# Two sums of a Strassen step in PSUM, split inputs of the second run by transfer, and a new placing of weight blocks and restores

## The chip, the cores and the metric

The kernel runs on one core of a Trainium2 chip. The metric is the device time of one execution in microseconds (us), taken as the median of several runs.

## The reference, cut to what matters

Three steps follow each other. The first is a retention (attention without softmax, with a decay by head) over q, k, v of 4 x 8 x 576 x 64, which gives x with 2304 rows of 512. The other two are:

```
h = x @ w_in                        # 512 -> 2048
g = where(h > 0, h, exp(min(h, 0)) - 1)
x = g @ w_out                       # 2048 -> 512
gate = 1 / (1 + exp(-(x @ w_gate))) # 512 -> 1536
val = x @ w_val
out = gate * val @ w_o2             # 1536 -> 512
```

The weights come in double precision, and the kernel works in single precision throughout.

## The kernel before, in words

**Numbers.** Every operand of a matmul is a pair of a high and a low part: ScalarE (ACT) copies the number to the high part, and VectorE (DVE) or GpSimd (POOL) subtracts it for the low part. A product takes three matmuls: high by high, high by low, low by high. A weight block comes from DRAM as words of doubles and is turned into such a pair on the chip by a chain of steps (`Weight.chain`): ACT, L149 and L150; DVE, L152, L153, L156 and L158; then the split, ACT L104 and POOL L105.

**Rows of x.** They lie in five groups: 0 to 3 with 512 columns each, group 4 with 256. Groups 0 and 1 form a pair, and so do 2 and 3.

**The unit.** For a pair and two column blocks of weights, `unit` does a 2 by 2 Strassen-Winograd step: seven products P1, P7, P6, P2, P5, P3, P4, in this order, of six 128x512 matmuls each, in three PSUM banks A, D, B, and eight sums. Its sums need three weight combinations in an `s` tile (`Sums.chain`, L188 to L192) and, for the pair, the split x pieces "11", "21", "22", "t1" to "t4" (`Pair`: `sum` at L436, `high` at L440, `low` at L444). The sums spoken of below are c22 (L493, from s4 and bank D), c21 (L505, from s2 and bank D), and the copy of A to B at L474. After a unit of the first feed-forward layer, `elu` finishes each of four results: two ACT steps (L526, L527) and one DVE step (L528), which reads the source of the result a second time. Its tiles and the PSUM banks are written "e" and "u" in the profile.

**The order.** Everything is written out by hand: the engines' queues hold their instructions in the order of the program. The stages are: retention with a first pass over part of the first layer (to 175 us), the **first run** of the first layer (pair 0 and 1, six units q = 2 to 7, each followed by `small_a` for group 4, whose matmuls go to bank B), the **second run** (pair 2 and 3, the same six units, whose weights are fetched from DRAM by `restore`, L874), and the second layer, twelve units f for pair 0 and 1 (with conversions of weights) and twelve for pair 2 and 3. Between the products of a unit stand calls of `bg`, which take the next entries of a plan (conversions of weights, saves at L865, restores), and of `fill(j)`, which issue at place j the down projections of the last unit (`down_a`, evacuated by DVE at L597; `down`, evacuated at L633) and the unit's hooks. Hooks remake the split x pieces of the next pair with `sum` and `split` from f32 rows, which are reloaded from DRAM (L815) or stand in y. In the second run the weight blocks of the four f in `EARLY` are converted ahead and parked.

Of the kernel before, what the change touches and what calls it, by code (L numbers as in the profile page):

```python
# [36 lines left out]
EARLY = (0, 1, 4, 7)  # L37
# [14 lines left out]
def retention_elu_glu(  # L52
# [149 lines left out]
    for f in range(FB):  # L202
        for i, (n, src) in enumerate((("g", w_gate), ("v", w_val), ("2", w_o2))):
            if f in EARLY:
                two = EARLY.index(f) % 2
                W[n, f] = Weight(src[f], (0, 1, 1)[i] ^ two, i, parked)
            else:
                W[n, f] = Weight(src[f], SLOT[n](f), i + 3 * (i < 2 and f in (3, 6, 8, 10)))
        home = (lambda: parked_sums) if f in EARLY else (lambda f=f: s_tile(f % 2))
        W["s", f] = Sums(W["v", f], W["g", f], home)  # L210
# [201 lines left out]
    class Pair:  # L412
# [7 lines left out]
        def __init__(self, g, out_by=None, sums=None):  # L420
            self.g, self.out_by = g, out_by
            self.x, self.sums = {}, y_of if sums is None else sums
# [6 lines left out]
        def f32(self, name):  # L429
            g, k = {"11": (0, 0), "t1": (0, 0), "t2": (0, 0), "21": (0, 1), "t4": (0, 1), "12": (1, 0), "t3": (1, 0),  # L430
                    "22": (1, 1)}[name]
            return self.sums[self.g + g][:, k * 1024 : k * 1024 + 1024]
# [37 lines left out]
    def unit(pair, ws, bg, fill, banks, mid, ends, explicit=False):  # L470
# [22 lines left out]
        dve.tensor_tensor(out=s4, in0=s4, in1=D, op=ALU.add)  # L493
# [3 lines left out]
        mid(1, 1, s4)  # L497
# [33 lines left out]
    def unit_a(pair, q, bg, fill):  # L531
# [7 lines left out]
        unit(pair, ws, bg, fill, [u_bank(i) for i in range(3)], mid, lambda *_: None, True)  # L539
# [100 lines left out]
    with tc.manual_schedule():  # L640
# [133 lines left out]
        early = []  # L774
        for i in range(0, len(EARLY), 2):
            f0, f1 = EARLY[i : i + 2]
            early += [("g", f0), ("v", f0), ("s", f0), ("2", f0), ("2", f1), ("g", f1), ("v", f1), ("s", f1)]
        feed += [W[n] for n in early if n[0] != "s"]
# [3 lines left out]
        feed, last_ones = deque(feed), [W["o", FA - 2], W["o", FA - 1], W["2", FB - 1]]  # L782
# [34 lines left out]
        def remake(p, at):  # L817
            return dict(zip(at, (
                [lambda: p.split("11", pool)],
                [lambda: p.sum("t1"), lambda: p.sum("t3")],  # L820
                [lambda: p.split("t3", pool)],
                [lambda: p.split("t1", dve), lambda: p.sum("t2")],
                [lambda: p.split("21", pool)],
                [lambda: p.split("t2", dve)],
            )))

        def remake_more(p, *rest):
            return {0: [lambda: p.split("22", dve), lambda: p.sum("t4"), *rest[:1]], 2: [lambda: p.split("t4", dve)], 3: list(rest[1:])}
# [78 lines left out]
        for s in range(end):  # L907
# [38 lines left out]
            save()  # L946
            if s == begins[1] + 8:
# [41 lines left out]
        def plan_a(q):  # L989
# [4 lines left out]
            if q > Q0:  # L994
                parts += [(("o", 2 * q), (4, 6, 7, 8, 10)), (("o", 2 * q + 1), (9, 11, 13, 14, 16))]
# [4 lines left out]
        def plan_b(f):  # L1000
            have = lambda f: f < FB and f not in EARLY
            parts = []
            if have(f + 1):
                parts += [(("v", f + 1), (0, 2, 3, 4, 5) if f == 1 else (0, 1, 3)), (("g", f + 1), (0, 2, 3, 4, 6) if f > 1 else (2, 5, 6, 7, 8)),
                          (("s", f + 1), (8, 9, 11) if f > 1 else (10, 11, 12))]
            if have(f):
                parts += [(("2", f), (2, 5, 6, 7, 9))]
            if f and have(f + 2):
# [3 lines left out]
        def filler(places, bg, hooks):  # L1012
            def fill(j):
# [3 lines left out]
                for at in (j, j + 0.5):  # L1017
                    for h in hooks.get(at, ()):
                        if h:
                            h()  # L1020
# [14 lines left out]
        for i in range(0, len(EARLY), 2):  # L1035
            f0, f1 = EARLY[i : i + 2]
            ahead.append(((("g", f0), (0, 2, 3, 4, 6)), (("v", f0), (3, 5, 6, 7, 9)), (("s", f0), (12, 13, 15)),
# [173 lines left out]
```

## Time and profile before

| what | value |
|---|---|
| time, median of 3 runs (lowest to highest) | 930.71 us (929.28 to 931.34) |
| the profiled execution: its own time, its span | 930.19 us, 928.4 us |
| TensorE (PE) busy in the span | 879.3 us, 95% |
| DVE busy | 626.4 us, 67% |
| ACT busy | 447.7 us, 48% |
| POOL busy | 380.9 us, 41% |
| mean granted TensorE clock | 0.988 |

The span runs from the first instruction to the last. A clock of 1.00 stands for the full rate, 2.4 GHz; where it is granted at 1.2 GHz a row shows 0.5. A busy PE in half-clock stretches counts in full, so that what the clock costs is to be read beside the busy time.

### The profile page before, as it was taken

What the parts mean: (1) busy time and instruction counts of PE and PEld (TensorE: products, weight loads), DVE (VectorE), ACT (ScalarE), POOL (GpSimd) and SP (SyncE); (2) the same over time, 40 slices, a digit from 0 to 9 for tenths busy, and PEclk for the clock granted to TensorE, in tenths of its full rate; (3) what the DMA queues carried; (4) which work ended last, traced back from release to release, by engine and by line L of the source; (5) the groups of instructions that cost most, each with busy time, mean ns of one, the idle gap of its engine ahead of it and who ended that gap; (6) DMA issues with size and microseconds to landing.
All of it is one profiled execution on the core that took longest, in us unless ns stands there. A gap on an engine that the chain in (4) does not pass through costs nothing.

```text
span 928.4 us, 15685 instructions
## 1 busy us (share of the span) xinstructions
PE 879.3 (95%) x6250; PEld 733.0 (79%) x6250; DVE 626.4 (67%) x876; ACT 447.7 (48%) x807; POOL 380.9 (41%) x290
## 2 busy tenths in 40 slices
PE   7889999899999969999988999999999899999998
PEld 5789998678877858777766788888888788888886
DVE  3767657879999697777786766857996732333334
ACT  2345565567666555646663554535553422323221
POOL 2255536456545563445462443434554511212121
PEclk9999999999999989999999999999999999999999
DMA  9877626535463737787782784464557466535322
GB/s 342 248 229 212 174 69 237 217 130 204 146 222 119 299 110 269 262 303 273 251 311 95 250 286 159 158 237 160 193 191 270 157 226 231 204 136 199 141 113 91
DMA packets 62233, 188.50 MB, mean 203 GB/s; under 512 B 9808, under 2 KB 19024, under 8 KB 55760
## 3 DMA queue, kind: packets, MB, share of 16 engines
q1 hardware_dynamic: 60752, 186.01, 57.3%
q10 hardware_dynamic: 1408, 1.49, 0.5%
q8 instruction: 49, 0.80, 0.4%
q14 instruction: 24, 0.20, 0.1%
HBM read 124.05 MB, written 63.44 MB: 202 GB/s over the span
## 4 chain that ended last, share of the span: by engine, by line
PE 62%; DVE 19%; ACT 7%; issue 5%; DMA 4%; POOL 3%; ACTq 0%; SPq 0%; DVEq 0%; POOLq 0%
PE u L109 10%; PE u L111 10%; PE u L110 10%; PE acc L109 7%; PE acc L110 7%; PE acc L111 7%; PE to L257 3%; DVE e L528 2%; PE tile L109 2%; PE tile L110 2%; PE tile L111 2%; PE h L356 2%; DVE y L436 2%; DVE t L156 2%; DVE t L152 2%
## 5 line engine op out<-in xcount | busy, mean ns | idle before, releaser
L105 POOL TENSOR_TENSOR g<-e,g 128x512 fp32r<-128x512 f32 x104 | 144.8, 1398 | 324.1 <-ACT g L104 256.3
L109 PE MATMUL u<-x,s 128*128 128x512 f32 x288 | 116.2, 403 | 6.4 <-ACT e L492 2.4
L111 PE MATMUL u<-x,s 128*128 128x512 f32 x288 | 114.7, 398 | 0.7 <-POOL s L105 0.7
L110 PE MATMUL u<-x,s 128*128 128x512 f32 x288 | 114.4, 397 | 0.0
L633 DVE TENSOR_TENSOR y<-y,acc 128x512 f32<-128x512 f32 x90 | 61.0, 684 | 70.4 <-PE acc L111 70.0
L104 ACT CAST g<-e 128x512 fp32r<-128x512 f32 x104 | 64.1, 621 | 83.9 <-DVE e L546 65.5
L109 PE MATMUL u<-x,w 128*128 128x512 f32 (+1 forms) x264 | 99.0, 375 | 3.7 <-DVE e L528 1.8
L110 PE MATMUL u<-x,w 128*128 128x512 f32 (+1 forms) x264 | 98.6, 374 | 0.0
L111 PE MATMUL u<-x,w 128*128 128x512 f32 (+1 forms) x264 | 98.3, 372 | 0.0
L109 PE MATMUL acc<-w,g 128*128 128x512 f32 x192 | 75.4, 393 | 2.6 <-DVE y L633 2.6
L110 PE MATMUL acc<-w,g 128*128 128x512 f32 x192 | 75.4, 392 | 0.0
L111 PE MATMUL acc<-w,g 128*128 128x512 f32 x192 | 75.3, 392 | 0.0
L109 PEld LDWEIGHTS u<-x,s 128*128 128x128 f32 x288 | 54.6, 190 | 22.8 <-ACT e L492 3.2
L105 POOL TENSOR_TENSOR w<-t,w 128x512 fp32r<-128x512 f32 x37 | 50.6, 1369 | 49.1 <-ACT w L104 43.4
L111 PEld LDWEIGHTS u<-x,s 128*128 128x128 f32 x288 | 54.7, 190 | 14.6 <-POOL s L105 1.3
L110 PEld LDWEIGHTS u<-x,s 128*128 128x128 f32 x288 | 54.9, 191 | 12.8
L109 PE MATMUL acc<-g,w 128*128 128x512 f32 (+1 forms) x176 | 60.6, 345 | 1.7 <-ACT w L104 0.6
L109 PEld LDWEIGHTS u<-x,w 128*128 128x128 f32 x264 | 50.1, 190 | 13.8 <-DVE e L493 2.7
L597 DVE TENSOR_TENSOR y<-y,tile 128x512 f32<-128x512 f32 x76 | 51.2, 680 | 14.5 <-PE tile L111 14.2
L111 PE MATMUL acc<-g,w 128*128 128x512 f32 (+1 forms) x176 | 60.3, 342 | 0.3 <-DVE w L105 0.2
L110 PE MATMUL acc<-g,w 128*128 128x512 f32 (+1 forms) x176 | 60.2, 342 | 0.0
L493 DVE TENSOR_TENSOR e<-e,u 128x512 f32<-128x512 f32 x36 | 24.6, 684 | 51.3 <-ACT e L492 51.3
(172 smaller groups left out, 2201.0 us busy)
## 6 DMA issues: line engine op xcount, KB each, us to landing
w<-c SPq DMA_DIRECT2D x72, 512.0 KB, 5.8
c<-w SPq DMA_DIRECT2D x48, 512.0 KB, 4.9
s<-c SPq DMA_DIRECT2D x22, 1024.0 KB, 8.1
c<-s SPq DMA_DIRECT2D x18, 1024.0 KB, 5.0
in<-in_ain SPq DMA_DIRECT2D x12, 1024.0 KB, 5.6
y<-y SPq DMA_DIRECT2D x8, 1024.0 KB, 5.7
raw<-in_w_out SPq DMA_DIRECT2D x14, 512.0 KB, 4.2
c<-x SPq DMA_DIRECT2D x12, 512.0 KB, 6.5
```

The source lines that it names most:

```text
L104: act.copy(hi, src)
L105: lo_engine.tensor_tensor(out=lo, in0=src, in1=hi.bitcast(F32), op=ALU.subtract)
L109: pe.matmul(out_, wh, xh, start=start, stop=False, skip_group_check=shared)
L110: pe.matmul(out_, wh, xl, start=False, stop=False, skip_group_check=shared)
L111: pe.matmul(out_, wl, xh, start=False, stop=stop, skip_group_check=shared)
L152: dve.tensor_scalar(out=f, in0=f, scalar1=LEAST, scalar2=MOST, op0=ALU.max, op1=ALU.min)
L156: add_engine.tensor_tensor(out=t, in0=t, in1=low, op=ALU.add)
L257: return pe.matmul(out_, w, x, start=start, stop=True, skip_group_check=True)
L356: pe.matmul(h, w[:, a, c[k]], x[:, b, k, t], start=i + k == 0, stop=i == 2 and k == KB - 1)
L493: dve.tensor_tensor(out=s4, in0=s4, in1=D, op=ALU.add)
L597: dve.tensor_tensor(out=y, in0=y, in1=a, op=ALU.add)
L633: dve.tensor_tensor(out=o, in0=o, in1=a, op=ALU.add)
```

## The change

The sum c22 is written to bank B in both runs of the first layer, and c21 to bank D in the first run. `low` on POOL is done in two instructions of half the width. The pieces "11", "21" and "22" of the second pair, which are split once already for the first pass, are stored to DRAM (3 x 1 MB) and fetched in the last unit of the first run; before they were split a second time from f32 rows. The remaining hooks there and in the two later remakes are placed anew. `EARLY` is (0, 1, 6, 11) for (0, 1, 4, 7), and its blocks have a regular plan. Restores of a second-run unit start with the `s` tile. The four down projections of the first unit stand at places 2, 3, 4, 4 for 0, 2, 4, 4; the last first-run unit converts its two `o` blocks earlier; the plan of the second layer is the same for every f, and closing the extra buffers and unparking y are one f earlier.

```diff
-EARLY = (0, 1, 4, 7)
+EARLY = (0, 1, 6, 11)
...
         def low(self, name, engine):
             p = self.x[name]
-            engine.tensor_tensor(out=p[:, 1], in0=self.src, in1=p[:, 0].bitcast(F32), op=ALU.subtract)
+            if engine is dve:
+                dve.tensor_tensor(out=p[:, 1], in0=self.src, in1=p[:, 0].bitcast(F32), op=ALU.subtract)
+                return
+            for k in range(KH):
+                engine.tensor_tensor(out=p[:, 1, k], in0=self.src[:, k], in1=p[:, 0, k].bitcast(F32), op=ALU.subtract)
+
+        def store(self, name):
+            g, k = {"11": (0, 0), "21": (0, 1), "22": (1, 1)}[name]
+            self.halves[name] = dpool.tile([128, 2, KH, 512], F32, tag=f"h{name}", name="h")
+            sp.dma_start(out=self.halves[name], in_=x_of[self.g + g][:, :, k * KH : k * KH + KH, :].bitcast(F32))
+
+        def fetch(self, name):
+            sp.dma_start(out=self.place(name).bitcast(F32), in_=self.halves[name])
...
-        dve.tensor_tensor(out=s4, in0=s4, in1=D, op=ALU.add)
+        c22 = B if explicit else s4
+        dve.tensor_tensor(out=c22, in0=s4, in1=D, op=ALU.add)
         mid()
         bg()
         fill(4)
-        mid(1, 1, s4)
+        mid(1, 1, c22)
...
-        dve.tensor_tensor(out=s2, in0=s2, in1=D, op=ALU.add)
+        c21 = D if to_d else s2
+        dve.tensor_tensor(out=c21, in0=s2, in1=D, op=ALU.add)
         bg()
         fill(6)
-        mid(1, 0, s2)
+        mid(1, 0, c21)
...
-        def remake(p, at):
-            return dict(zip(at, (
-                [lambda: p.split("11", pool)],
-                [lambda: p.sum("t1"), lambda: p.sum("t3")],
-                [lambda: p.split("t3", pool)],
-                [lambda: p.split("t1", dve), lambda: p.sum("t2")],
-                [lambda: p.split("21", pool)],
-                [lambda: p.split("t2", dve)],
-            )))
+        def remake(p):
+            return {
+                1: [lambda: p.split("11", dve)],
+                2: [lambda: p.sum("t1"), lambda: p.sum("t3")],
+                4: [lambda: p.split("t3", pool), lambda: p.split("t1", dve), lambda: p.sum("t2")],
+                5: [lambda: p.split("21", pool)],
+                6: [lambda: p.split("t2", dve)],
+            }
...
+            for i, n in enumerate(("11", "21", "22")):
+                if s == begins[1] + 2 + i:
+                    second.store(n)
...
-                parts += [(("o", 2 * q), (4, 6, 7, 8, 10)), (("o", 2 * q + 1), (9, 11, 13, 14, 16))]
+                early_o = ((0, 1, 2, 3, 5), (2, 4, 5, 6, 8)), ((4, 6, 7, 8, 10), (9, 11, 13, 14, 16))
+                parts += [(("o", 2 * q + i), early_o[q + 1 < QN][i]) for i in range(2)]
...
-                        hooks = remake(second, (3, 4, 5, 5.5, 6, 7))
-                    at = (0, 1, 2, 3, 4, 4, 6, 6, 7, 7) if len(todo) > 4 else (0, 2, 4, 4)
+                        p = second
+                        hooks = {
+                            0: [lambda: p.fetch("11")],
+                            3: [lambda: p.fetch("21"), lambda: p.sum("t1"), lambda: p.sum("t3")],
+                            4: [lambda: p.split("t3", pool), lambda: p.sum("t2")],
+                            5: [lambda: p.fetch("22"), lambda: p.split("t2", dve), lambda: p.sum("t4")],
+                            6: [lambda: p.split("t1", pool)],
+                            7: [lambda: p.split("t4", dve)],
+                        }
+                    at = (0, 1, 2, 3, 4, 4, 6, 6, 7, 7) if len(todo) > 4 else (2, 3, 4, 4)
...
-                    for n, i in zip(back, (1, 3, 5, 7, 9)):
+                    for n, i in zip(back[-1:] + back[:-1], (0, 2, 4, 6, 8)):
                         plan[i] = [*plan[i], lambda n=n: restore(n)]
                     if q + 1 == QN:
-                        hooks = remake(y_pair, (0, 2, 3, 4, 5, 6))
+                        hooks = remake(y_pair)
...
-            (0, FB - 1): remake(p1, (3, 4, 5, 5.5, 6, 7)),
-            (1, 0): remake_more(p1, None),
+            (0, FB - 1): remake(p1),
+            (1, 0): remake_more(p1),
```

The change moves instructions on the queues. **An ordinary unit of the first run, queue of DVE**, from the finish of c22 to the evacuations after the next unit's P1 (L528 finishes a result, L505 is c21, L597 an evacuation). Before:

```order
L528 SCALAR_TENSOR_TENSOR e<-e 128x512
L528 SCALAR_TENSOR_TENSOR e<-e,u 128x512
L152 TENSOR_SCALAR more<-more 128x512
L153 TENSOR_SCALAR more<-more 128x512
L505 TENSOR_TENSOR e<-e,u 128x512
L156 ISA more<-raw,more 128x1024
L597 TENSOR_TENSOR y_875<-y_875,tile 128x512
L158 SCALAR_TENSOR_TENSOR more<-raw,more 128x512
L528 SCALAR_TENSOR_TENSOR e<-e 128x512
L528 SCALAR_TENSOR_TENSOR e<-e,u 128x512
L597 TENSOR_TENSOR y_2330<-y_2330,tile 128x512 x2
```

After, the same place (line 543 is the old 528, 520 the old 505, 612 the old 597):

```order
L543 SCALAR_TENSOR_TENSOR e<-e,u 128x512 x2
L152 TENSOR_SCALAR more<-more 128x512
L153 TENSOR_SCALAR more<-more 128x512
L520 TENSOR_TENSOR u<-e,u 128x512
L156 ISA more<-raw,more 128x1024
L612 TENSOR_TENSOR y_875<-y_875,tile 128x512
L158 SCALAR_TENSOR_TENSOR more<-raw,more 128x512
L543 SCALAR_TENSOR_TENSOR e<-e,u 128x512 x2
L612 TENSOR_TENSOR y_2330<-y_2330,tile 128x512 x2
```

The order is the same, and the two finishing steps that read e alone now read e and a bank.

**The last unit of the first run, queue of DVE**, from c22 to the first evacuation after P4 (y_875). Before:

```order
L493 TENSOR_TENSOR e<-e,u 128x512
L158 SCALAR_TENSOR_TENSOR t<-raw,t 128x512
L436 TENSOR_TENSOR y_3925<-y_3927,y_3925 128x1024
L436 TENSOR_TENSOR y_3927<-y_3927 128x1024
L528 SCALAR_TENSOR_TENSOR e<-e 128x512
L528 SCALAR_TENSOR_TENSOR e<-e,u 128x512
L152 TENSOR_SCALAR t<-t 128x512
L153 TENSOR_SCALAR t<-t 128x512
L444 TENSOR_TENSOR x_114<-y_3925,x_114 128x1024
L436 TENSOR_TENSOR y_3925<-y_3927,y_3925 128x1024
L505 TENSOR_TENSOR e<-e,u 128x512
L156 ISA t<-raw,t 128x1024
```

After (L437 and L446 are the old L436 and L444, L507 is the old L493), from two sums ahead of c22 to y_875:

```order
L437 TENSOR_TENSOR y_3933<-y_3935,y_3933 128x1024
L437 TENSOR_TENSOR y_3935<-y_3935 128x1024
L507 TENSOR_TENSOR u<-e,u 128x512
L437 TENSOR_TENSOR y_3935<-y_3935,y_3933 128x1024
L543 SCALAR_TENSOR_TENSOR e<-e,u 128x512 x2
L446 TENSOR_TENSOR x_114<-y_3935,x_114 128x1024
L437 TENSOR_TENSOR y_3933<-y_3933,y_3935 128x1024
L520 TENSOR_TENSOR u<-e,u 128x512
L612 TENSOR_TENSOR y_875<-y_875,tile 128x512
```

The conversion of a weight block (L152, L153, L156) is gone from this place, three sums and one low part remain in front of L520 behind c22, and the first two sums now stand ahead of c22.

**A middle unit of the second run, queue of SP**, from one unit's first restore on (w<-c a weight block, s<-c an `s` tile, c<-x_113 and c<-s saves). Before:

```order
L874 DMA w<-c 128x1024 x2
L865 DMA c<-x_113 128x1024
L874 DMA w<-c 128x1024
L865 DMA c<-x_113 128x1024
L874 DMA w<-c 128x1024
L874 DMA s<-c 128x2048
```

After:

```order
L885 DMA s<-c 128x2048
L876 DMA c<-s 128x2048
L885 DMA w<-c 128x1024 x2
L876 DMA c<-x_113 128x1024
L885 DMA w<-c 128x1024 x4
```

The `s` tile of the next unit moves from the end of a unit's restores to their start.

## Rows read from the trace of the kernel before

**Rows 1.** Page, part 1: busy time, share of the span and instructions of each engine.

```profile
PE 879.3 (95%) x6250; PEld 733.0 (79%) x6250; DVE 626.4 (67%) x876; ACT 447.7 (48%) x807; POOL 380.9 (41%) x290
```

**Rows 2.** Windows: start and end, length, busy of PE, PEld, DVE, ACT, POOL, clock, DMA.

```profile
176.70:205.00 28.30, 24.35 (x109) 19.24 (x109) 20.79 (x32) 16.63 (x30) 11.45 (x9) 0.94 0.39 130
205.00:232.00 27.00, 25.97 (x136) 21.87 (x135) 26.64 (x34) 18.96 (x33) 18.16 (x13) 1.00 0.55 187
312.50:344.40 31.90, 24.22 (x121) 20.09 (x121) 24.24 (x23) 16.37 (x26) 17.51 (x9) 0.93 0.56 213
344.40:370.00 25.60, 25.60 (x117) 21.77 (x118) 20.02 (x27) 14.44 (x23) 7.73 (x6) 0.89 0.75 267
474.00:500.00 26.00, 19.52 (x80) 14.36 (x79) 22.96 (x24) 15.24 (x22) 13.96 (x8) 1.00 0.62 242
700.00:740.00 40.00, 37.40 (x179) 31.12 (x178) 29.49 (x34) 18.88 (x31) 22.75 (x13) 0.96 0.59 211
```

**Rows 3.** All instructions of line 528 by operands: nanoseconds, shortest, median, longest.

```profile
L528 DVE SCALAR_TENSOR_TENSOR e<-e,u x30: 674/686/689, 189.5 to 484.8; 128x512 f32<-128x512 f32 x30
L528 DVE SCALAR_TENSOR_TENSOR e<-e x24: 678/691/1791, 196.8 to 489.4; 128x512 f32<-128x512 f32 x24
```

**Rows 4.** Timeline of PE and DVE, second unit: start, duration, instruction, [idle before, releaser].

```profile
219.29 0.68 DVE L528 SCALAR_TENSOR_TENSOR e<-e 128x512 f32<-128x512 f32 x1
220.51 0.28 PE L109 MATMUL u<-x,w 128*128 128x256 f32 x1
225.70 1.79 DVE L528 SCALAR_TENSOR_TENSOR e<-e 128x512 f32<-128x512 f32 x1
228.01 1.27 DVE L597 TENSOR_TENSOR y<-y,tile 128x512 f32<-128x512 f32 x2
228.83 0.47 PE L109 MATMUL tile<-g,w 128*128 128x512 f32 x1 [1.03 <-ACT u L474]
```

**Rows 5.** Timeline of PE, ACT and DVE, first unit of the first run.

```profile
178.88 0.50 PE L109 MATMUL tile<-g,w 128*128 128x512 f32 x1 [2.14 <-DVE e L371]
179.44 0.58 ACT L474 COPY u<-u 128x512 f32<-128x512 f32 x1
194.78 0.28 PE L109 MATMUL u<-x,w 128*128 128x256 f32 x1
196.83 0.70 DVE L528 SCALAR_TENSOR_TENSOR e<-e 128x512 f32<-128x512 f32 x1 [1.29 <-ACT e L527]
```

**Rows 6.** Timeline of POOL, DVE and PE, last unit of the first run.

```profile
323.47 2.41 POOL L444 TENSOR_TENSOR x<-y,x 128x1024 fp32r<-128x1024 f32 x1 [7.88 <-ACT x L440]
323.62 2.54 DVE L153 TENSOR_SCALAR t<-t 128x512 uint32<-128x512 uint32 x1
336.44 2.30 DVE L444 TENSOR_TENSOR x<-y,x 128x1024 fp32r<-128x1024 f32 x1
338.78 2.17 DVE L436 TENSOR_TENSOR y<-y,y 128x1024 f32<-128x1024 f32 x1
341.47 2.24 DVE L156 CUSTOM_DVE_ANT_0 t<-raw,t 128x1024 uint16<-128x1024 uint16 x1
344.36 0.58 PE L109 MATMUL tile<-x,w 128*128 128x256 f32 x1 [7.17 <-DVE y L597]
```

**Rows 7.** DMA issues from 300 to 350 us: count, KB each, median us to landing.

```profile
y<-x SPq DMA_DIRECT2D x2, 1024.0 KB, 9.7
```

**Rows 8.** Timeline of SP's queue and PE, second run.

```profile
385.12 0.45 SPq L874 DMA_DIRECT2D s<-c  x1
395.99 0.47 PE L109 MATMUL u<-x,s 128*128 128x512 f32 x1 [1.56 <-DVE t L158]
```

**Rows 9.** Timeline of DVE and PE, unit f = 11 of the second layer.

```profile
721.36 2.60 DVE L444 TENSOR_TENSOR x<-y,x 128x1024 fp32r<-128x1024 f32 x1 [1.47 <-ACT x L440]
723.99 2.19 DVE L436 TENSOR_TENSOR y<-y,y 128x1024 f32<-128x1024 f32 x1
727.43 0.51 PE L109 MATMUL acc<-w,g 128*128 128x512 f32 x1 [2.60 <-DVE y L633]
```

More of the change, by code (lines that the diff above doesn't have):

```diff
@@ L204, in retention_elu_glu @@
             if f in EARLY:
-                two = EARLY.index(f) % 2
-                W[n, f] = Weight(src[f], (0, 1, 1)[i] ^ two, i, parked)
+                W[n, f] = Weight(src[f], i % 2, i, parked)
             else:
-                W[n, f] = Weight(src[f], SLOT[n](f), i + 3 * (i < 2 and f in (3, 6, 8, 10)))
+                W[n, f] = Weight(src[f], SLOT[n](f), i + 3 * (i < 2 and f in (3, 5, 7, 9)))
         home = (lambda: parked_sums) if f in EARLY else (lambda f=f: s_tile(f % 2))
@@ L421, in __init__ @@
             self.g, self.out_by = g, out_by
-            self.x, self.sums = {}, y_of if sums is None else sums
+            self.x, self.sums, self.halves = {}, y_of if sums is None else sums, {}
         def place(self, name):
@@ L431, in f32 @@
                     "22": (1, 1)}[name]
+            if self.halves and name == "t2":
+                g, k = 1, 1
             return self.sums[self.g + g][:, k * 1024 : k * 1024 + 1024]
@@ L468, in finish_later, with unit @@
             later.pop(0)()
-    def unit(pair, ws, bg, fill, banks, mid, ends, explicit=False):
+    def unit(pair, ws, bg, fill, banks, mid, ends, explicit=False, to_d=False):
         A, D, B = banks
@@ L538, in unit_a @@
         ws = W["i", 2 * q], W["i", 2 * q + 1], W["z", q]
-        unit(pair, ws, bg, fill, [u_bank(i) for i in range(3)], mid, lambda *_: None, True)
+        unit(pair, ws, bg, fill, [u_bank(i) for i in range(3)], mid, lambda *_: None, True, to_d)
     def unit_b(pair, f, bg, fill):
@@ L773, in retention_elu_glu @@
                 feed += [W["o", 2 * q], W["o", 2 * q + 1]]
[L774 to L778, printed above, removed]
+        early = [(n, f) for f in EARLY for n in "gv2"]
+        feed += [W[n] for n in early]
         for f in range(FB):
@@ L1003, in plan_b @@
             if have(f + 1):
-                parts += [(("v", f + 1), (0, 2, 3, 4, 5) if f == 1 else (0, 1, 3)), (("g", f + 1), (0, 2, 3, 4, 6) if f > 1 else (2, 5, 6, 7, 8)),
-                          (("s", f + 1), (8, 9, 11) if f > 1 else (10, 11, 12))]
+                parts += [(("v", f + 1), (0, 1, 3)), (("g", f + 1), (0, 2, 3, 4, 6)), (("s", f + 1), (8, 9, 11))]
             if have(f):
                 parts += [(("2", f), (2, 5, 6, 7, 9))]
-            if f and have(f + 2):
+            if have(f + 2):
                 parts += [(("v", f + 2), (11, 13))]
@@ L1016, in fill @@
                     bg()
[L1017 to L1020, printed above, removed]
+                for h in hooks.get(j, ()):
+                    h()
             return fill
@@ L1034, in retention_elu_glu @@
         ahead = []
[L1035 to L1040 removed]
+        for f in EARLY:
+            ahead.append(((("g", f), (0, 2, 3, 4, 6)), (("v", f), (3, 5, 6, 7, 9)), (("s", f), (11, 12, 14)),
+                          (("2", f), (10, 13, 14, 15, 17))))
+        ahead = planned(7 + 72 + 13, *((n, [7 + 18 * i + a for a in at]) for i, part in enumerate(ahead) for n, at in part))
         y_pair = Pair(0, [sp])
@@ L1060, in retention_elu_glu @@
                     if q == Q0:
-                        hooks = remake_more(second, None, unpark)
+                        hooks = {0: [unpark]}
                         at = (1, 2, 3, 4, 4, 5, 5, 6, 6, 7)
@@ L1107, in retention_elu_glu @@
                         more()
+                    if f == FB - 3:
+                        close()
                     if f == FB - 2:
-                        close()
-                    if f == FB - 1:
                         unpark((2, 3))
```

13 lines of the change are left out of this document (5 added, 8 removed).

## The prediction, made before the changed kernel ran

> **What bounds the kernel now.** I read the page's busy line first: PE is busy 879.3 of 928.4 us, 95%, no other engine over 67% [rows 1]. PE is the bound, and the change leaves its matmuls as they are. So the change can only win where PE waits, or where its clock is lowered after a wait. I then listed PE's gaps in the timeline and looked behind each for the instruction that ended last; the stretches in which most of them lie are in the windows [rows 2]. Their columns are read in pairs: length minus PE busy is the wait, and (1 - clock) times the length is what the clock costs on top. From 205 to 232 PE is busy 25.97 of 27.00 us and DVE 26.64, so DVE has no room there. From 312.5 to 344.4 PE waits 7.7 us and the clock takes 0.07 x 31.9 = 2.2 us, and in the next stretch another 0.11 x 25.6 = 2.8 us without any wait. From 474 to 500 PE waits 6.5 us.
>
> **The ordinary units of the first run.** In units two to five PE stops once, about 1.0 us each, right after the next unit's P1. The row names the ACT copy of A to B, which is done by then; what ends last is the evacuation behind a finish by L528 that took 1.79 us [rows 4]. L528 comes in two forms: with one operand in a bank it takes 674 to 689 ns in all 30 cases, with both in e 678 to 1791 in 24 [rows 3]. The long ones are those with POOL at work beside them. Writing c21 to D gives this finish a bank to read. It ends 1.1 us earlier, the evacuation with it, and the gap of 1.03 us goes: four such units, -4 us. The bounds are -4.1 and 0 (if another instruction ends at the same time).
>
> The price: c22 now lies in B, and B is the bank that `small_a` writes right after. Its first matmul must wait for the finish of c22. In the second unit that finish starts at 219.29 and takes 0.68, so ends at 219.97, and `small_a` starts at 220.51 [rows 4]: 0.5 us of room, and no cost as long as the sums on DVE keep their pace. No DVE write to PSUM is in this trace. The nearest rows are ACT's copy within PSUM, 0.58 us [rows 5], and DVE's finish that reads a bank, 0.69 [rows 3]; neither is longer than its neighbours, so I take no difference, with 0.5 us per write as the bad end.
>
> The Trainium skill speaks against this place ("Perfetto Trace Analysis", section "Optimizing Scalar/DVE Operations"): DVE's overhead per instruction is about 60 ns on SBUF and about 125 ns on PSUM. By it 18 sums written and 18 finishes read in PSUM would add 36 x 65 ns = 2.3 us of DVE time, an estimate from that page. The trace does not show it for reads: 686 ns with a bank and 691 ns without at the median [rows 3].
>
> **The first unit.** Here PE waits 2.14 us before the first down projection, for the last finish of the pass before [rows 5]; the window 176.7 to 205 holds 3.95 us of waits and 0.06 x 28.3 = 1.7 us of clock [rows 2]. With the down projections at 2, 3, 4, 4, P7 goes first, but P6 writes A and so waits for the copy of A, which ends at 179.44 + 0.58 = 180.02. From the end of P1 at 178.88 - 2.14 = 176.74 that is 3.3 us, and P7 fills less than half of it: a gap of about 2 us remains, so this edit gains 0.1 us. Against that, this unit has no down projection between P4 and `small_a`, which starts at 194.78, while the finish of c22 ends at 196.83 + 0.70 = 197.53 [rows 5]. That is a new wait of 2.75 us. Returned of it are at most the other waits of this window, 3.95 - 2.14 = 1.8, since those behind `small_a` are for the same finishes. Net -0.1 + 2.75 - 1.8 = +0.8. The bounds are -1.7, if the clock no longer falls, and +2.5, if it falls once more.
>
> **The last unit of the first run.** The wait of 7.17 us is for an evacuation (L597) at the end of a queue on DVE: low part 2.30, sum 2.17, c21, a step of a conversion 2.24 [rows 6]. With c21 (about 0.7 as L528 on a bank [rows 3]) these come to 7.4 us. The change takes the conversion to earlier places, and takes pieces "11", "21" and "22" out of all three engines (POOL loses two low parts of about 2.4 us each, DVE one). In front of the evacuation there remain behind c22 one sum, two short finishes, one low part, one sum, c21. DVE's single-input step L153 took 2.54 us while POOL did one 1024-wide low part of 2.41 us, and both ended together [rows 6]: DVE sat out the whole POOL instruction. Two halves of it would let DVE in after about 1.2 us, so a jam costs DVE half as much. I expect the evacuation to be due within 1 us of PE, and then little clock is lost. The loss today is 7.17 + 2.2 + 2.8 = 12.2 us; I take 1.2 as staying, -11. Bounds: -12.2 if all goes, -6 if half the wait stays and the clock drops after it.
>
> The fetches are three transfers of 1 MB and their stores another three. The nearest row, two loads of 1 MB in the same stretch, lands 9.7 us after issue with much ahead of it [rows 7]. "11" is issued some 20 us before P1 of the second run needs it, "21" and "22" later but for later products: hidden, 0. If "11" came after P1 was due, each us would be one us of PE. The stores lie in the retention stage, where SP's queue waits for nothing of theirs.
>
> **The second run.** The wait of 1.56 us at 394.4 is put down to DVE, but the matmul's weight is an `s` tile whose restore was issued at 385.12 behind the others and is late [rows 8]; a smaller one of the same kind follows in the next unit. With `s` first in the queue, -2 in all (bounds -2 and +1, when the `o` or `i` blocks are late instead). In the last unit and the first of the second layer PE waits 6.5 us between 474 and 500 [rows 2], behind remakes of 1024-wide sums and low parts on DVE. With "11" on DVE and done first, and POOL's low parts in halves, I take -5; bounds -6.5 and -2.
>
> **Second layer.** At f = 11 PE waits 2.60 us for an evacuation behind a low part of 2.60 and a sum of 2.19 [rows 9], and the clock costs 0.04 x 40 = 1.6 [rows 2]. In the new order both stand one product (P3) earlier, the two sums ahead of them two places earlier, and no conversion is left in this unit: -4, bounds -4.2 and 0. The same conversions are done in other f, where the list of PE's gaps has none over 0.2 us from f = 2 on: 0.
>
> **The sum.** 0.8 - 4 - 11 - 2 - 5 - 4 = -25.2. New waits (a finish read late in D ahead of P7, c22 behind two sums in the last unit, `small_a` now and then) I set at +2, about what the room of 0.5 us in rows 4 can cost in four units: -23.2. 930.2 - 23.2 = 907.0 for the profiled execution, which is 0.5 below the median of 930.7; so 907.5 us.
>
> **The rivals.**
> *DVE is the bound of the ordinary units* (for: 26.64 of 27.00 us busy [rows 2]; against: each unit sheds over 1 us of it). Then `small_a` waits for c22 as the next unit waited for the evacuation, and -4 goes: 911.5 us. Chance 0.15.
> *The jam at the end of the first run moves instead of going* (for: two sums and a low part are still in front of c21, and c22 itself stands behind two sums, so P4, which writes D, waits for it; against: the conversion and one low part leave). Half of the term goes, 5.5: 913 us. 0.15.
> *The second run is held by transfers* (for: three more MB, and the restores share a queue with saves; against: rows 8 are the largest such wait). The -2 and half of the -5 go: 912 us. 0.12.
> *Slower: DVE's write to PSUM is dear.* 18 sums are written there, and DVE has no room in the first run. If each took d longer and PE waited for all of it, the gain is used up at d = 23.2 / 18 = 1.3 us; at d = 1.5 the time is 907.5 + 27 = 934.5 us. Against it stands the ACT copy within PSUM at 0.58 us [rows 5]. 0.04.
> *The change does nothing for the time,* because "11" lands late. All terms but that of the jam come to -12.2; the jam's 12.2 would have to be 24.4, so with 5 us of clock as today P1 would wait 19 us. "11" would take some 39 us to land, four times rows 7: about 930.5 us. 0.03.
> The forecast has the rest, 0.51.
>
> **Range and chances.** 899 to 919. The good ends of all bounds come to -1.7 - 4.1 - 12.2 - 2 - 6.5 - 4.2 = -30.7, 900 us, and I leave 1 us for small gaps that I did not count. The high end is two of the first three rivals together and some of the bad end of the second layer. A measurement of this kernel can tell about 0.2%, 2 us, from no change. All cases but the last two are faster by more than that; I keep a little for mishaps that I do not see: faster 0.90, same 0.04, slower 0.06.
>
> **What would show it.** Right: L528's new forms all near 0.69 us; no gap after P1 in units three to six; the wait at 337 under 2 us and no half-clock stretch of 10 us behind it; no wait for an `s` tile in the second run; f = 11 without a wait over 1 us. A new row of PE before the 256-wide matmuls of `small_a` in unit one, 2 to 3 us, with DVE's finish as its releaser. Wrong: such a row in every unit; DVE sums to a bank over 1 us; PE waiting for a fetched piece; a long wait in P4 of the last unit.

## The result, and the profile after

The changed kernel took 902.92 us in the median of 4 runs (901.97 to 904.38), the kernel before 930.02 in the median of 4: a ratio of 0.9708 with a 95% interval of 0.9689 to 0.9728, faster by 27 us. The forecast was 907.5 in a range of 899 to 919. The profiled execution has a span of 900.5 us, 27.9 us less than before.

PE's busy share on the page went from 95% [rows 1] to 97%, with the same number of matmuls:

```profile
PE 869.6 (97%) x6250; PEld 729.4 (81%) x6250; DVE 612.8 (68%) x876; ACT 444.0 (49%) x804; POOL 379.0 (42%) x295
```

PE's busy time is 9.7 us shorter although its work is the same. About two thirds of that is the clock: in four stretches whose mean clock was 0.90 to 0.99 before and is 1.00 after (retention, the last unit of the first run, the unit behind it, and f = 11) PE's busy time fell by 6.5 us. The other 3.2 us lie in stretches of unchanged clock, most of them stretches whose waits went; what made them was not traced.

To see where the time came from I took the start of P1's first matmul of each unit from PE's timeline in both traces, and subtracted. What a stretch gained is the change from one row to the next:

| stretch (P1 to P1) | forecast, us | measured, us |
|---|---|---|
| retention, up to the first unit | 0 | -1.0 |
| first unit, and what it gives back in the second | +0.8 | +1.4 - 0.9 = +0.5 |
| the four waits of 1.0 us behind P1 | -4 | -4.4 |
| last unit of the first run, and the clock behind it | -11 | -8.6 - 1.3 = -9.9 |
| second run, second to fifth unit | -2 | -1.1 |
| last unit of the second run, first of the second layer | -5 | -3.75 - 1.6 = -5.4 |
| units f = 1 and 2 of the second layer | 0 | -2.2 |
| unit f = 11 | -4 | -4.4 |
| new waits, not placed | +2 | 0 beside those in the rows above |
| all | -23.2 | -27.9 |

The windows cut at these starts (columns as in [rows 2]):

```profile
174.23:199.10 24.87, 20.07 (x92) 16.60 (x90) 19.07 (x28) 13.57 (x24) 10.73 (x9) 0.93 0.44 154
306.03:333.58 27.55, 27.09 (x141) 22.54 (x139) 23.13 (x28) 16.36 (x28) 19.06 (x13) 1.00 0.98 382
333.58:357.25 23.67, 23.67 (x116) 19.79 (x115) 15.85 (x22) 12.03 (x21) 9.62 (x7) 1.00 0.73 288
443.44:465.90 22.46, 21.18 (x91) 16.56 (x89) 19.83 (x24) 13.69 (x22) 12.17 (x9) 1.00 0.78 290
465.90:491.37 25.47, 24.11 (x115) 19.72 (x116) 18.24 (x22) 12.14 (x18) 7.18 (x5) 1.00 0.26 107
699.76:716.51 16.75, 16.75 (x74) 13.56 (x73) 10.14 (x13) 6.46 (x11) 4.26 (x3) 1.00 0.61 220
```

The last unit of the first run (306.03) waits 0.5 us in all, and its DMA share is 0.98; f = 11 (699.76) waits nowhere. The first unit waits 4.8 us.

All instructions of the finish (line 543, the old 528) and of the two sums that are now written to a bank, by operands, in nanoseconds, shortest, median, longest:

```profile
L543 DVE SCALAR_TENSOR_TENSOR e<-e,u x48: 672/681/690, 185.1 to 465.2; 128x512 f32<-128x512 f32 x48
L543 DVE SCALAR_TENSOR_TENSOR e<-e x6: 679/691/1743, 359.9 to 469.3; 128x512 f32<-128x512 f32 x6
...
L507 DVE TENSOR_TENSOR u<-e,u x12: 682/683/697, 187.1 to 458.6; 128x512 f32<-128x512 f32 x12
...
L520 DVE TENSOR_TENSOR u<-e,u x6: 681/682/690, 195.6 to 330.7; 128x512 f32<-128x512 f32 x6
```

The 18 finishes that moved to a bank lie with the others between 672 and 690 ns, whatever POOL does; of the six that are left one still takes 1743 and one 1.16 us, both while POOL is at work. A sum written to a bank takes 682 or 683 ns at the median.

The first unit, timeline of PE and DVE:

```profile
179.23 0.51 PE L109 MATMUL u<-x,s 128*128 128x512 f32 x1 [2.08 <-ACT u L487]
193.89 0.69 DVE L543 SCALAR_TENSOR_TENSOR e<-e,u 128x512 f32<-128x512 f32 x1 [1.24 <-ACT e L542]
194.63 0.39 PE L109 MATMUL u<-x,w 128*128 128x256 f32 x1 [2.72 <-DVE e L543]
```

Both waits that were forecast are there: about 2 us at P6 for the copy of A, and 2.72 us (2.75 forecast) ahead of `small_a` for the finish of c22.

The last unit of the first run, DVE in front of the evacuation (line 612, the old 597), and the matmul that needs it:

```profile
327.21 1.35 DVE L446 TENSOR_TENSOR x<-y,x 128x1024 fp32r<-128x1024 f32 x1 [0.26 <-ACT x L441]
328.48 2.31 DVE L437 TENSOR_TENSOR y<-y,y 128x1024 f32<-128x1024 f32 x1
330.72 0.68 DVE L520 TENSOR_TENSOR u<-e,u 128x512 f32<-128x512 f32 x1
331.31 0.67 DVE L612 TENSOR_TENSOR y<-y,tile 128x512 f32<-128x512 f32 x1
332.04 0.39 PE L109 MATMUL tile<-x,w 128*128 128x256 f32 x1
```

The evacuation ends at 331.98 and PE's matmul starts at 332.04. The wait of 7.17 us [rows 6] is gone with nothing to spare. Behind c22 two sums and one low part stand in front of this c21; the section on the change says three sums, and the prediction has it right.

The fetched pieces come later than the nearest row of before let expect (9.7 us [rows 7]), but no wait of PE is for one:

```profile
x<-h SPq DMA_DIRECT2D x3, 1024.0 KB, 14.4
```

So the rival in which "11" lands late is out: its fetch is issued 21 us before P1 of the second run, and P1 starts without a wait.

The second run has waits of a new kind, third and fourth unit, ACT and PE:

```profile
380.91 0.62 ACT L104 CAST x<-t 128x512 fp32r<-128x512 f32 x1 [4.60 <-DMA c<-x]
383.26 0.50 PE L109 MATMUL u<-x,s 128*128 128x512 f32 x1 [0.87 <-ACT u L487]
402.96 0.67 ACT L149 ACTIVATE t<-raw 128x512 f32<-128x512 f32 x1 [4.30 <-DMA raw<-in_w_val]
405.90 0.50 PE L109 MATMUL u<-x,s 128*128 128x512 f32 x1 [1.60 <-ACT u L487]
```

ACT stands still for 4.6 and 4.3 us in the conversion of early blocks: first because the home of a block is still being saved to DRAM (c<-x), then because raw words have not landed. The copy of A to B stands behind, and P6 waits for it.

Unit f = 11, DVE:

```profile
692.21 1.98 DVE L446 TENSOR_TENSOR x<-y,x 128x1024 fp32r<-128x1024 f32 x1
694.23 2.20 DVE L437 TENSOR_TENSOR y<-y,y 128x1024 f32<-128x1024 f32 x1
697.54 1.27 DVE L648 TENSOR_TENSOR y<-y,acc 128x512 f32<-128x512 f32 x2
```

The low part and the sum of [rows 9] are there, but end at 696.4, ahead of what P4 and the evacuations need.

### The profile page after: what moved, and what is told of

Its sections match the earlier page's. It is cut to its first block, busy times and chain, and to the rows that moved or that the text cites. A ratio compares the mean times of both kernels' runs of the same rounds, so it can differ in the third digit from the quotient of the medians.

```text
span 900.5 us, 15728 instructions
## 1 busy us (share of the span) xinstructions
PE 869.6 (97%) x6250; PEld 729.4 (81%) x6250; DVE 612.8 (68%) x876; ACT 444.0 (49%) x804; POOL 379.0 (42%) x295
## 4 chain that ended last, share of the span: by engine, by line
PE 77%; DVE 11%; ACT 6%; DMA 2%; POOL 2%; issue 2%; ACTq 0%; DVEq 0%; POOLq 0%; SPq 0%
PE u L109 12%; PE u L111 12%; PE u L110 12%; PE acc L109 8%; PE acc L110 8%; PE acc L111 8%; PE tile L109 3%; PE to L256 3%; PE tile L110 3%; PE tile L111 3%; PE h L355 2%; DVE t L153 1%; DMA c<-x 1%; DVE t L156 1%; ACT x L441 1%
## 5 line engine op out<-in xcount | busy, mean ns | idle before, releaser
L109 PEld LDWEIGHTS u<-x,s 128*128 128x128 f32 x288 | 54.1, 188 | 20.0 <-ACT u L487 5.9
L111 PEld LDWEIGHTS u<-x,s 128*128 128x128 f32 x288 | 54.1, 188 | 13.2
L110 PEld LDWEIGHTS u<-x,s 128*128 128x128 f32 x288 | 54.1, 188 | 12.7
L505 ACT COPY e<-u 128x512 f32<-128x512 f32 x36 | 21.1, 587 | 82.9 <-PE u L111 82.9
```

The costliest lines, as they stand in the source:

```text
L109: pe.matmul(out_, wh, xh, start=start, stop=False, skip_group_check=shared)
L110: pe.matmul(out_, wh, xl, start=False, stop=False, skip_group_check=shared)
L111: pe.matmul(out_, wl, xh, start=False, stop=stop, skip_group_check=shared)
L505: act.copy(s4, A)
```

## The experiments

Each starts from the changed kernel. "Table" means the starts of P1 as above, against those of the changed kernel's profile. Two things in that profile are not in most others: the wait of 1.60 us for raw words in the fourth unit of the second run (all runs below but two gain 1.87 us there), and in the first unit the clock fell once, while in eight of nine other kernels with the same two waits it fell after each, 3.41 us at half rate, which makes the first unit 1.2 to 1.6 us longer. The start of the first unit also moves by up to 3 us between runs (174.0 to 177.4 us) with nearly the same program ahead of it, so that the -1.0 in the table's first row means nothing. The kernel before took 929.44 us (median of 7), 933.79 (one run) and 929.73 (median of 9) beside the three sets of experiments, so that single times differ by more than some of the effects; where they do, the table decides.

**The two sums in SBUF again.**

```diff
-        c22 = B if explicit else s4
+        c22 = s4
...
-        c21 = D if to_d else s2
+        c21 = s2
```

> The changed kernel with c22 and c21 written to SBUF as before; all else as changed. Theory (a finish with both operands in SBUF is held up beside POOL): about 1.1 us come back after P1 in each of units three to six, and the new wait of 2.7 us ahead of small_a in the first unit goes, of which some 1.4 us turn up elsewhere in that unit; with what the second run loses, +3 us, 905 to 907 us. Rival (DVE's length per unit is what counts, not which finish is slow): the waits come back only in part, 902 to 903 us.

906.26 us, ratio to before 0.9746 (0.9728 to 0.9764). Third unit, DVE and PE:

```profile
224.20 1.79 DVE L543 SCALAR_TENSOR_TENSOR e<-e 128x512 f32<-128x512 f32 x1
227.33 0.48 PE L109 MATMUL tile<-g,w 128*128 128x512 f32 x1 [1.04 <-ACT u L487]
```

The finish takes 1.79 us again and the wait behind P1 is back in each of the four units: +1.1 four times in the table, and +0.4 more in the last unit. The wait ahead of `small_a` is gone; the first unit is 1.7 us shorter and the second 0.9 longer. This is the theory, by its numbers.

The second run loses as well, most of it in its last unit, +1.15 us, where the finish of c22 takes its full length beside POOL again:

```profile
467.11 1.75 DVE L543 SCALAR_TENSOR_TENSOR e<-e 128x512 f32<-128x512 f32 x1
469.51 0.51 PE L109 MATMUL u<-x,w 128*128 128x512 f32 x1 [2.00 <-DVE e L543]
```

The wait there is 0.91 us in the changed kernel. So the sum in bank B has a share in the gain at the end of the second run, which the prediction put down to the remake and to POOL's halves.

**Pieces split again; `o` blocks late; both.** The first takes out the stores and fetches and puts back the hooks of before; the second is one line; the third has both.

```diff
-                        hooks = {
-                            0: [lambda: p.fetch("11")],
...
+                        hooks = {
+                            3: [lambda: p.split("11", pool)],
+                            4: [lambda: p.sum("t1"), lambda: p.sum("t3")],
+                            5: [lambda: p.split("t3", pool), lambda: p.split("t1", dve), lambda: p.sum("t2")],
+                            6: [lambda: p.split("21", pool)],
+                            7: [lambda: p.split("t2", dve)],
+                        }
...
-                parts += [(("o", 2 * q + i), early_o[q + 1 < QN][i]) for i in range(2)]
+                parts += [(("o", 2 * q + i), early_o[1][i]) for i in range(2)]
```

> The changed kernel without the stores and fetches of 11, 21 and 22: the second pair's pieces are split a second time from f32 rows, at the places of before, with low parts on POOL in halves and the o blocks converted early as changed. Theory (the jam on DVE and POOL at the end of the first run is made by both the split pieces and the conversion): a wait of 2 to 5 us for an evacuation in the last unit comes back, and 1 to 3 us in the first unit of the second run, 906 to 911 us. Rival (the conversion alone made the jam): under 1 us, 903 to 904 us.

> The changed kernel with the last first-run unit's two o blocks converted at the places of before; fetches kept. Theory (both made the jam): the conversion step in front of the evacuation brings back a wait of 2 to 4 us, 905 to 907 us. Rival (the split pieces alone made the jam): 902.5 to 903.5 us.

> The changed kernel with both edits at the end of the first run undone: pieces split a second time, and the o blocks converted at the places of before. Alone the first gave back 1.0 us in the last unit and the one after, the second 4.1 us. Theory (one queue on DVE that is too long; what it is over by is PE's wait): together they give back more than their sum, 7 to 10 us with what the clock takes after a long wait. Rival (two separate waits): their sum, 5 us.

904.06 us (0.9717, 0.9696 to 0.9739), 908.07 us (0.9771, 0.9749 to 0.9793), and 909.70 us in one run. First, PE in the last unit with pieces split again:

```profile
336.76 0.39 PE L109 MATMUL tile<-x,w 128*128 128x256 f32 x1 [1.43 <-DVE y L612]
```

With the `o` blocks late, DVE and PE there:

```profile
337.68 1.15 DVE L156 CUSTOM_DVE_ANT_0 t<-raw,t 128x1024 uint16<-128x1024 uint16 x1
339.48 0.39 PE L109 MATMUL tile<-x,w 128*128 128x256 f32 x1 [3.09 <-DVE y L612]
```

With both:

```profile
332.35 2.32 DVE L446 TENSOR_TENSOR x<-y,x 128x1024 fp32r<-128x1024 f32 x1
339.19 0.58 PE L109 MATMUL tile<-x,w 128*128 128x256 f32 x1 [4.52 <-DVE y L612]
```

By the table the last unit and the one after it lose 1.0, 4.1 and 7.1 us. The first is short of its expectation: 1.43 us of wait for 2 to 5, and 0.2 us in the next unit for 1 to 3. At 904.06 us it lies by the time alone within the noise of the changed kernel, at the edge of its rival. The second has the wait of "both made the jam" (3.09 us for 2 to 4), and another of 1.38 us in P4, for c22. The third is over the sum of 5.1, at the low end of what one queue should give. The waits ahead of this matmul add (1.43 + 3.09 = 4.52); what comes on top is the clock, which falls to half for 6.83 us behind the long wait, 5.9 of them under PE's work, and fell in neither of the other two.

What an edit is worth thus depends on whether the other is there. The place of the conversion is worth 4.1 us alone and 7.1 - 1.0 = 6.1 on top of the transfers; the transfers are worth 1.0 alone and 7.1 - 4.1 = 3.0 on top of the conversion. Both together account for 7.1 of the 9.9 us that this place gained; the sums in banks are 0.4 of the rest, as above, and what the remainder belongs to was not tried.

**The first unit's down projections at 4, 4, 6, 6.**

```diff
-                    at = (0, 1, 2, 3, 4, 4, 6, 6, 7, 7) if len(todo) > 4 else (2, 3, 4, 4)
+                    at = (0, 1, 2, 3, 4, 4, 6, 6, 7, 7) if len(todo) > 4 else (4, 4, 6, 6)
```

> The changed kernel with the first unit's four down projections at places 4, 4, 6, 6, so that two of them stand between P4 and small_a. Theory (the wait of 2.7 us is there because nothing lies between P4 and small_a): it goes but for some tenths, and PE does not wait more elsewhere, 900 to 901 us. Rival (the chain of ACT and DVE behind the finishes sets the pace of this unit): the wait moves to P3 or to the next unit's P1, 902.5 to 903.5 us.

898.93 us (0.9666, 0.9641 to 0.9692). `small_a` starts without a wait:

```profile
193.06 0.28 PE L109 MATMUL u<-x,w 128*128 128x256 f32 x1
```

The table gives -2.9 us for the first unit and no change to the next. So the new wait was a matter of what lies between P4 and `small_a`, and the rival falls. The expectation that PE waits no more elsewhere did not hold in this trace: the third unit of the second run takes 2.5 us more, with a wait of 1.85 us and a fall of the clock behind it. It is the wait that the best version below removes.

**Restores of the second run with the `s` tile last.**

```diff
-                    for n, i in zip(back[-1:] + back[:-1], (0, 2, 4, 6, 8)):
+                    for n, i in zip(back, (1, 3, 5, 7, 9)):
```

> The changed kernel with the restores of the second run in the order of before, the s tile last. Theory (the s tile was late because it was last): a wait of 1.2 to 1.6 us for an s tile in the second or third unit of the second run and one of about 0.5 us in a later one come back, +1.5 to 2 us over the changed kernel, in these units. Rival (the second run is held by something else that comes due at the same time): the table by unit moves by less than 0.5 us.

910.96 us in one run. SP's queue and PE in the second run:

```profile
376.14 0.44 SPq L885 DMA_DIRECT2D s<-c  x1
386.51 0.47 PE L109 MATMUL u<-x,s 128*128 128x512 f32 x1 [2.21 <-DMA s<-c]
```

Three units now wait for an `s` tile or what stands behind it, 2.21, 1.48 and 1.75 us, and the clock falls after the first. By the table the second run is 3.7 us longer, or 5 to 6 if the wait for raw words in the changed kernel's profile is left out. The mechanism is the one expected, and two to three times as large. That the rest of the change puts more on this queue would explain the size, but was not tried.

**The last pair's remake at the places of before; POOL's low parts whole; both.**

```diff
-            (0, FB - 1): remake(p1),
+            (0, FB - 1): {3: [lambda: p1.split("11", pool)], 4: [lambda: p1.sum("t1"), lambda: p1.sum("t3")],
+                          5: [lambda: p1.split("t3", pool), lambda: p1.split("t1", dve), lambda: p1.sum("t2")],
+                          6: [lambda: p1.split("21", pool)], 7: [lambda: p1.split("t2", dve)]},
...
-            if engine is dve:
-                dve.tensor_tensor(out=p[:, 1], in0=self.src, in1=p[:, 0].bitcast(F32), op=ALU.subtract)
+            if True:
+                engine.tensor_tensor(out=p[:, 1], in0=self.src, in1=p[:, 0].bitcast(F32), op=ALU.subtract)
```

> The changed kernel with the remake for the last pair at the places of before (3, 4, 5, 5, 6, 7), still with no conversion in unit f = 11. Theory (the place of the sums and low parts makes the wait of f = 11): 2.6 us of wait and up to 1.7 us of clock come back in that unit, 905.5 to 907.5 us. Rival (the conversions in that unit made it): under 0.5 us, 902.5 to 903.5 us.

> The changed kernel with POOL's low parts in one 1024-wide instruction. Theory (DVE sits out the whole POOL instruction): DVE steps beside these take 2.2 to 2.6 us again, and 0.5 to 1.5 us come back in each of the last units of the first run, the second run and at f = 11, where they fall into a tight place: +1 to 3 us. Rival (these low parts now lie where DVE has room): under 0.5 us in all.

> The changed kernel with the remake for the last pair at the places of before, and POOL's low parts in one instruction; no conversions in unit f = 11. Alone the first gave back 1.2 us there, the second nothing. Theory (three edits each take about 1.1 us off the same queue, and the clock falls after a long wait only): a wait of 1.3 to 1.7 us at f = 11, 2.2 to 3.5 us in all. Rival (the whole low parts do nothing): 1.2 us as with the first alone.

One run each: 903.79, 904.52 and 901.15 us. At f = 11, with the old places alone:

```profile
697.10 1.47 DVE L446 TENSOR_TENSOR x<-y,x 128x1024 fp32r<-128x1024 f32 x1 [1.47 <-ACT x L441]
702.05 0.50 PE L109 MATMUL acc<-w,g 128*128 128x512 f32 x1 [0.40 <-DVE y L648]
```

and with the old places and whole low parts:

```profile
693.87 2.60 DVE L446 TENSOR_TENSOR x<-y,x 128x1024 fp32r<-128x1024 f32 x1 [1.47 <-ACT x L441]
699.95 0.50 PE L109 MATMUL acc<-w,g 128*128 128x512 f32 x1 [1.52 <-DVE y L648]
```

With whole low parts on POOL a DVE low part beside them takes 2.60 us as before [rows 9], with halves 1.47, and PE's wait differs by the same 1.1 us. Of the 2.60 us of before another 1.1 is left by difference, 2.60 - 1.52, for what else left this unit, the conversions above all, and 0.4 is the places. The conversions were not put back alone: `EARLY` and the earlier unparking of y stand in every run. In the table f = 11 costs 1.2 and 1.8 us in these runs (4.4 in the kernel before): the clock fell in neither. The whole low parts alone cost nothing there and under 0.2 us in the other two places that the expectation named, so that its rival holds. The first expectation was wrong on both sides, theory and rival; the last was right on the wait and too high by the clock. So three edits took from one queue: with the conversions gone the clock stayed up, and either of the other two takes most or all of the wait that is left.

**The first pair's remake at the places of before.** 
```diff
-                        hooks = remake(y_pair)
+                        hooks = {0: [lambda: y_pair.split("11", pool)], 2: [lambda: y_pair.sum("t1"), lambda: y_pair.sum("t3")],
+                                 3: [lambda: y_pair.split("t3", pool)], 4: [lambda: y_pair.split("t1", dve), lambda: y_pair.sum("t2")],
+                                 5: [lambda: y_pair.split("21", pool)], 6: [lambda: y_pair.split("t2", dve)]}
```

> The changed kernel with the remake for the first pair at the places of before (0, 2, 3, 4, 5, 6) in the last unit of the second run; conversions as changed. Theory (the remake's place makes the waits there): 2 to 4 us come back from the last unit of the second run to the first of the second layer. Rival (the early blocks' conversions made them, and they are over by then in the changed kernel): under 1 us.

904.63 us in one run; the table shows less than 0.3 us there. A wait appears, and those of 0.37 and 0.91 us go:

```profile
461.58 0.50 PE L109 MATMUL u<-x,s 128*128 128x512 f32 x1 [1.65 <-ACT e L505]
```

So with the conversions over by then, the remake's places alone gain nothing. What they are worth with the conversions still there was not tried.

**The early blocks' conversions in the places of before.** `EARLY` stays (0, 1, 6, 11); the order of loads, the homes and the plan are those of before.

```diff
-        for f in EARLY:
-            ahead.append(((("g", f), (0, 2, 3, 4, 6)), (("v", f), (3, 5, 6, 7, 9)), (("s", f), (11, 12, 14)),
-                          (("2", f), (10, 13, 14, 15, 17))))
+        for i in range(0, len(EARLY), 2):
+            f0, f1 = EARLY[i : i + 2]
+            ahead.append(((("g", f0), (0, 2, 3, 4, 6)), (("v", f0), (3, 5, 6, 7, 9)), (("s", f0), (12, 13, 15)),
+                          (("2", f0), (10, 14, 15, 16, 18)), (("2", f1), (22, 24, 25, 26, 28)),
+                          (("g", f1), (24, 27, 28, 29, 31)), (("v", f1), (28, 30, 31, 32, 34)), (("s", f1), (36, 37, 39))))
```

> The changed kernel with the early blocks (still f = 0, 1, 6, 11) loaded, homed and placed in the second run as before, so that their conversions go on through the last unit. Theory (these conversions, not the remake's places, made the waits from the last unit of the second run to the second unit of the second layer): 3 to 6 us come back there by the table of units. Rival (another edit took them away): under 0.5 us there.

909.83 us in one run. Last unit of the second run, DVE and PE:

```profile
470.04 2.19 DVE L438 TENSOR_TENSOR y<-y,y 128x1024 f32<-128x1024 f32 x1
473.48 0.50 PE L109 MATMUL u<-x,w 128*128 128x512 f32 x1 [2.77 <-DVE e L544]
```

4.0 us come back in that unit, within the expectation in size, but nothing in the two units after it, where the expectation had waits too; the two units before it lose 2.2 us more. DVE's last step of a conversion ends 18.6 us into that unit, and 6 us into it in the changed kernel. So the gain in the last unit (3.75 us) is there because the conversions are over earlier (plan, homes and loads were put back together, so which of them counts is open); the sum in bank B, put back alone above, is worth 1.15 us in the same unit, and the two overlap. The 1.6 us of the next unit came back in no run, and their cause is open.

**The best version.** Down projections at 4, 4, 6, 6, and the two homes of early blocks taken in turn.

```diff
-                W[n, f] = Weight(src[f], i % 2, i, parked)
+                W[n, f] = Weight(src[f], (i + EARLY.index(f)) % 2, i, parked)
```

> The changed kernel with the first unit's down projections at 4, 4, 6, 6 and the two homes of the early blocks taken in turn (the home of a block changes with its number), so that a home is written again 10 steps after its last block and not 7. Theory (ACT's queue stops at a home whose save to DRAM is not done, and the copy of A to B stands behind it): the wait of 1 to 2 us in the third unit of the second run goes, 896 to 898 us. Rival (the raw words of the next block are late as well): the wait stays, 898 to 900 us.

896.02 us in 5 runs (894.07 to 896.85), ratio to before 0.9632 (0.9619 to 0.9645), below the interval of the changed kernel. With the down projections at 4, 4, 6, 6 and the homes as changed, ACT had stood 5.67 us for a save at this place; now it goes on, and the second run has no wait from 350 to 420 us:

```profile
378.71 0.62 ACT L104 CAST x<-t 128x512 fp32r<-128x512 f32 x1 [5.67 <-DMA c<-x]
...
376.37 0.62 ACT L104 CAST x<-t 128x512 fp32r<-128x512 f32 x1 [1.44 <-DVE t L158]
...
350.00:420.00 70.00, 70.00 (x305) 57.00 (x304) 60.30 (x84) 44.50 (x79) 39.47 (x28) 1.00 0.81 287
```

The third unit is 3.7 us shorter than with the homes as changed, by this one edit. So the home that was written again too soon is shown as the cause of the wait in the third unit. The wait for raw words in the fourth is absent here as in nearly all runs and says nothing for either side.

## Why the prediction was right, point by point

- **The sums in banks.** Right in mechanism and size: 4.4 us for 4, and the first experiment gives back both the 1.79 us and the waits. A DVE sum written to PSUM takes what one written to SBUF does here, 682 or 683 ns for 687. The rival of a dear write is out, and so is that of DVE as the bound: `small_a` waited in the first unit only.
- **The first unit.** Both waits came to 0.1 us of what was worked out. The net was taken from one fall of the clock; in most runs it falls twice, which was the bad end of the bound. The good end was added up wrongly: 0.8 less 1.7 us of clock is -0.9 and not -1.7, and the good ends of all bounds come to -29.9 and not -30.7. Nothing else hangs on it. The edit of this unit cost time; the version at 4, 4, 6, 6 gives 2.9 us.
- **The end of the first run.** The direction was right and the wait went completely, where 1.2 us were to stay. The size of the term was off because the clock was counted wrongly: (1 - clock) times the length of 312.5 to 344.4 [rows 2] counts 2.2 us of lost clock in which PE stood still anyway, since all of the half clock in that window lies inside the wait. The table gives 9.9 us for what the prediction called 12.2. In a stretch that holds a wait, only the half clock under PE's work costs time. Without it the loss was 7.17 + 2.8 = 10.0 us. Both causes made the jam, as predicted, the conversion more than the transfers.
- **The second run.** -1.1 for -2: the wait for the `s` tile went, and waits of another kind took part of it, as ACT now stopped at a block's home and for raw words. The rival of transfers came true in this part, 0.87 and 1.60 us. The term for the end of the run was right in size (-5.4 for -5) and wrong in its reason, so its size is luck: put back alone, the remake's places do nothing there, while the conversions' later end costs 4.0 us and the sum in SBUF 1.15.
- **The second layer.** f = 11 right in size (-4.4 for -4). The prediction's reason, places and conversions, was a part; beside the old places the halves of POOL's low parts, which it had counted elsewhere, are worth another 1.1 us of wait. Where it had counted them, they gain nothing in the changed kernel. The 2.2 us in the units f = 1 and 2 were not in the sum: I had listed these waits (0.9, 0.5 and 0.7 us) and not seen that the new plan of the second layer starts these conversions one unit earlier. That this plan removes them is argued from the order only; it was not tried alone.
- **The rule on PSUM** ("Perfetto Trace Analysis" in the Trainium skill, section "Optimizing Scalar/DVE Operations") would have each of the moved instructions some 65 ns longer, an estimate from its figures: 2.3 us more of DVE's time in all. Measured, finishes on a bank take 681 ns and those on SBUF 691 at the median, sums to a bank 683 and to SBUF 687 in the second layer: the trace does not agree. The rule that did decide stands in "SBUF — State Buffer", section "Who interferes with whom": a DVE instruction with two inputs in SBUF contends with GpSimd's reads, one with at most one SBUF input outside the two-port modes does not. Here 48 finishes with one such input take at most 0.69 us, and of the six with two one takes 1.74: the trace agrees.
- **The total.** It came out 4.7 us beyond the forecast: 2.2 from the units f = 1 and 2, 2 from new waits that did not come on top, 1.0 from the first row, which means nothing. That the errors of the other terms (-0.4 to +1.1 each) cancel to half a microsecond is luck.

## What to carry to other kernels

A DVE instruction that reads two SBUF tiles beside a busy POOL can take 2.6 times as long; give it one operand from PSUM, or give POOL shorter instructions, when an evacuation stands behind it. A bank that takes on a result gets a new reader: look for the next matmul that writes the bank, and put PE work between. When a long wait is removed, ask which of several edits did it by putting back one and then two, since each can be worth more when the other is gone: here a conversion at the wrong place cost 4.1 us alone and 6.1 with the other edit undone, and the transfers that looked like the main thing 1.0 and 3.0.

## What was not expected of the hardware

The clock does not fall after every wait of the same length, and the length alone does not decide it. In the changed kernel's trace it stayed after the 2.08 us of the first unit and fell after the 2.72; in eight of nine others it fell after both. With the `o` blocks late it stayed after 3.09 us, while it fell after 1.85 us with the down projections at 4, 4, 6, 6 and after 1.80 with the early blocks as before. After 1.52 us at f = 11 it did not fall. The falls behind waits of 1.8 to 2.8 us are 3.41 us at half rate; behind 4.52 us it was 6.83, behind 7.17 it was 10.24. So an edit that shortens a wait can gain more than the difference: at f = 11 a wait of 1.52 us for 2.60 came with 2.6 us less in the table, 1.8 for 4.4.

A save to DRAM can hold up an engine and all that stands behind in its queue: ACT stood 4.6 us (5.67 in another run) because the tile it was to write was still being saved to DRAM, and PE lost 0.87 us (1.85) to the copy of A behind it.
